# Spreading a weight load over every fourth partition, with a half-made table, shared buffers and new instruction orders, in a two-layer spectral and mixer kernel

## The chip, the cores and the metric

The kernel runs on one core of one Trainium2 chip. The metric is the device time of one execution in microseconds (us). "Span" is the time from the first to the last instruction in a trace. In every execution for which both are on record the time is 1.7 to 2.2 us longer than the span. A kernel is timed several times, and each call of the experiments ran its kernels and the kernel before on the same chip. All timed runs here are in the fast state.

## The reference, cut to what matters

```python
def _A_ref(x, w_r, w_i):                  # x: 1 x 2048 x 512, w: 2048 x 257
    X = rfft2(x)                          # over the 2048 rows and the 512 columns
    return irfft2(X * (w_r + 1j * w_i))

def _B_ref(x, w1, w2, w3, w4):
    h = _gelu(_layernorm(x) @ w1)         # 512 x 512
    # ... four column groups of h shifted by -1, +1, -2, +2 rows ...
    x1 = x + hs @ w2
    return x1 + _gelu(_layernorm(x1) @ w3) @ w4      # 512 x 1792 and back

for _ in range(2):                        # written out twice in the original
    x = x + _A_ref(_layernorm(x), A_w_r, A_w_i)
    x = x + _B_ref(_layernorm(x), B_w1, B_w2, B_w3, B_w4)
```

All inputs are bf16. Both layers use the same weights.

## The kernel before

Each FFT is a chain of matmuls with constant tables. A layer runs through these stages, and three lists of short names fix the order in which they are issued. A name is an operation, an index, sometimes the engine of the eviction (the copy of a matmul's result out of PSUM, where the matmuls here write their `ps` tiles; A = ScalarE, V = VectorE), and after the dot a PSUM bank.

- front (`O`): transform over 128 points within the 2048, with the rows' 1/std folded into the table `Tq = T * rstd` (`Q`).
- `d`: transform of the 512 columns. `q`: the other factor of the 2048 rows, with the table `TL`. `p`: the weighing, VectorE products of `X` and `W` into buffers `PB`. `b`: the inverse of `q` with `TR`, evicted into `M`.
- `D`: inverse of `d`. `P`: inverse of the front. Then the mixer: `v`, `u` (w1, w2), `w`, `W` (w3, w4).

The weights `w_r` and `w_i` must lie on 128 partitions as two forward and two reversed copies. The kernel before loads 64 partitions and copies them to the other 64:

```python
def load_W(K, w, pl, lo, hi):
    v = w.rearrange("(m j) f -> m j f", j=64)[:, :, 1:257]
    j1 = max(lo, 1)
    K.nc.sync.dma_start(K.W[0:32, pl, lo:hi], v[:, lo:hi])
    K.nc.sync.dma_start(K.W[32:64, pl, j1:hi], v[:, 65 - hi:65 - j1][:, ::-1])
    # ...
    K.later.append(lambda: K.nc.gpsimd.dma_start(K.W[64:128, pl, lo:hi], K.W[0:64, pl, lo:hi]))
```

The squares for the layer norms write their unused full result to one single buffer, and the sum of squares comes from the accumulator:

```python
    def square(self, i, src):
        junk = K.stream.tile([P, D], BF16, name="junk", bufs=1)
        K.nc.scalar.activation(junk[:], src, ACT.Square, bias=0.0, scale=D ** -0.5, accum_out=self.s[:, i, 1:2])
```

The scaled tables of the front go to VectorE only where the letter is V:

```python
def scaled_T(K, q, r, eng="V"):
    K.Tq[q] = K.stream.tile([P, 2, P], BF16, name="Tq", bufs=12)
    if eng == "V":
        K.nc.vector.tensor_scalar(K.Tq[q][:], K.T[:], r, None, op0=ALU.mult)
    else:
        K.nc.scalar.activation(K.Tq[q][:], K.T[:], ACT.Copy, bias=0.0, scale=r)
```

While the first data are on their way, 44 matmuls on zeros (`WAKE = 44`) keep TensorE busy, from 1.01 to 8.01 us in the first profile.

Of the kernel before, what the change touches and what calls it, by code (L numbers as in the profile page):

```python
# [23 lines left out]
SLAB = 130  # L24
# [3 lines left out]
def dft_tables():  # L28
# [55 lines left out]
    TL = np.concatenate([-B, A, B], axis=3).transpose(1, 2, 0, 3).reshape(P, NB, 192)  # L84
# [3 lines left out]
    TR = TR.reshape(NH, P, 2, 64).transpose(1, 2, 0, 3)  # L88
# [63 lines left out]
def load_all(K, A_x, A_w_r, A_w_i, B_w1, B_w2, B_w3, B_w4):  # L152
# [15 lines left out]
    K.TL = K.const.tile(list(tabs["TL"].shape), BF16, name="TL")  # L168
    K.TR = K.const.tile([P, 3, NH, 64], BF16, name="TR")
    load_q = lambda k, sl: nc.sync.dma_start(getattr(K, k)[:, sl], dram[k][:, sl])  # L170
    load_q("TL", slice(0, 8))
    K.W = K.const.tile([P, 2, NH, 256], BF16, name="W")
    K.later = []
    for lo in range(0, NH, 8):
        for pl, w in enumerate((A_w_r, A_w_i)):
            load_W(K, w, pl, lo, lo + 8)
        if lo == 8:
            load_q("TL", slice(8, 16))
        if lo in (0, 16):
            nc.sync.dma_start(K.TR[:, 0:2, lo:lo + 16], dram["TR"][:, :, lo:lo + 16])  # L180
# [4 lines left out]
    def load_mlp():  # L185
        gate2 = K.const.tile([1, 16], BF16, name="gate2")
        nc.sync.dma_start(gate2[:], K.W[64:65, 1, NH - 1, 0:16])
        for k, w, n, c in (("w1", B_w1, 4, D), ("w2", B_w2, 4, D), ("w3", B_w3, 4, FH), ("w4", B_w4, 14, D)):
            t = K.const.tile([P, n, c], BF16, name=k)
            nc.sync.dma_start(t[:], w.rearrange("(t p) n -> p t n", p=P))  # L190
            setattr(K, k, t)
# [8 lines left out]
def load_W(K, w, pl, lo, hi):  # L200


    v = w.rearrange("(m j) f -> m j f", j=64)[:, :, 1:257]
    j1 = max(lo, 1)
    K.nc.sync.dma_start(K.W[0:32, pl, lo:hi], v[:, lo:hi])
    K.nc.sync.dma_start(K.W[32:64, pl, j1:hi], v[:, 65 - hi:65 - j1][:, ::-1])
    if lo == 0:
        K.nc.sync.dma_start(K.W[32:64, pl, 0], v[:, 32])
    K.later.append(lambda: K.nc.gpsimd.dma_start(K.W[64:128, pl, lo:hi], K.W[0:64, pl, lo:hi]))


def make_hT(K):
    K.hT = K.big.tile([P, 4, NQ * SLAB], BF16, name="hT")
    hv = K.hT[:].rearrange("p i (q c) -> p i q c", c=SLAB)
    K.nc.gpsimd.memset(hv[:, :, :, 0:1], 0.0)
    K.nc.gpsimd.memset(hv[:, :, :, SLAB - 1:SLAB], 0.0)
# [18 lines left out]
class Stats:  # L235
# [18 lines left out]
    def square(self, i, src):  # L254

        K = self.K
        junk = K.stream.tile([P, D], BF16, name="junk", bufs=1)
        K.nc.scalar.activation(junk[:], src, ACT.Square, bias=0.0, scale=D ** -0.5, accum_out=self.s[:, i, 1:2])  # L258
# [45 lines left out]
    def mean(self, i, src):  # L304
        K = self.K
        junk = K.stream.tile([P, D], BF16, name="junk", bufs=1)
        K.nc.scalar.activation(junk[:], src, ACT.Copy, bias=0.0, scale=1.0 / D, accum_out=self.s[:, i, 0:1])
# [83 lines left out]
def first_front(K):  # L391
# [44 lines left out]
    for f in K.later:  # L436
# [4 lines left out]
def layer(K, last):  # L441
# [5 lines left out]
    PB = K.grp.tile([P, 8, 2, 2, 256], BF16, name="PB", tag="gT")  # L447
    n_pab = [0]
    M = K.grp.tile([P, 2, 2, NQ, P], BF16, name="M", tag="gT")
    xn = K.big.tile([P, NQ, D], BF16, name="xn", tag="V_xn")  # L450
    hv = K.hT[:].rearrange("p i (q c) -> p i q c", c=SLAB)
    ps = {}
# [13 lines left out]
    def take_d(u, eng):  # L466
        n = len(UNITS[u])
        tv[u] = K.stream.tile([P, n, 512], BF16, name="TV", tag="TV_Y", bufs=3, padded_shape=[P, 2, 512])
# [7 lines left out]
    def over_q(u):  # L476
# [5 lines left out]
        for i, b in enumerate(bs):  # L482
            for t in range(2):
                for h in range(2):
                    r = slice(64 * h, 64 * h + 64)
                    nc.tensor.matmul(o[:, h, i * 256:(i + 1) * 256], lhsT=K.TL[r, b, 64 * (1 - t):64 * (3 - t)],  # L486
# [6 lines left out]
    def weigh(u):  # L493
# [3 lines left out]
        for pl in range(2):  # L497
            t = PB[:, n_pab[0] % 8]
            n_pab[0] += 1
            w = K.W[:, pl, 2 * u:2 * u + 2 * n].rearrange("p (n h) f -> p h n f", h=2)  # L500
# [28 lines left out]
    def take_D(m, eng):  # L529
        Y[m] = K.stream.tile([P, 2, 512], BF16, name="Y", tag="TV_Y", bufs=3, padded_shape=[P, 2, 512])  # L530
# [18 lines left out]
    def stats2(q):  # L549
        ln[q // 4].square(q % 4, K.x[:, q, :])  # L550
# [29 lines left out]
    def gelu1(k):  # L580
        g, h = divmod(k, 2)
        o = ps.pop(("v", k))
        for i in range(2):
            nc.scalar.activation(hv[:, 2 * h + i, 4 * g:4 * g + 4, 1:P + 1],  # L584
                                 o[:, i].rearrange("p (q c) -> p q c", q=4), ACT.Gelu_apprx_tanh, bias=0.0, scale=1.0)

    def w2(n):
        q = ROWS[n]
        ps["u", n] = o = banks(K, 1)[:, 0]
        for j, dq in enumerate((-1, 1, -2, 2)):  # L590
            qq = (q + dq) % NQ
            st = SLAB * qq + 1 + (q + dq - qq) // NQ
# [79 lines left out]
    def take_front(k, eng):  # L672
# [3 lines left out]
        if k < PLAIN:  # L676
            if eng == "A":
                ps["right", k] = K.stream.tile([P, 2, 256], FP32, name="right", tag="TV_Y", bufs=3)
# [6 lines left out]
    def permute(k):  # L685

        w = K.W[:, k // 8, 4 * (k % 8):4 * (k % 8) + 4]
# [9 lines left out]

    next_V = {}
    table = {"d": over_d, "t": take_d, "q": over_q, "x": take_q, "p": weigh, "b": back_q,
# [29 lines left out]
s0 s3 s2 s4 i0 i2 s1 s5 s6 f4 i3 i4 S0 s9 s10 J0 S4 i10 s13 s7 Q0V J4 Q2A f5 s8 O0 i7 Q1A Q3A i9 Q4A i8 S5 s11 S1  # L729
s12 G0A O1 J1 i11 i12 Q5V G1A J5 Q9V Q6V Q13V Q10V s14 S2 s15 O2 Q7V O6 Q8V i15 J2 i14 Q12V G2A G6A Q11V O4 S3 J3  # L730
Q15V O3 Q14V G4A O5 G3V O7 G5A O8 G8A G7V
"""
ORDER_A = """
d1.0 d0.1 d4.2 t1A t0V q0.0 x0V q1.4 d6.6 x1V t4A p0 d2.0 t6A q4.4 d10.2 t2V q6.6 x4A p1 N0 p4 d8.4 t10A t8V x6A p6
q2.0 b1.2 b4.3 m1A d12.6 b0.2 m4A d14.3 x2A q10.4 t12A p2 d15.0 b5.1 t14V x10A m0V q8.6 b2.3 b6.4 x8A m2A m6A m5A
q12.6 q14.2 N1 p10 b7.5 t15A p8 b10.4 m7V b11.1 b3.0 x12A m11A x14V p12 p14 m3A b8.5 m8A q15.6 m10A b9.2 x15A p15
b12.3 b13.5 m12A m9A b14.4 m13V b15.3 m15V m14A m15A D0.2 D1.4 Y1A Y0V D3.6 P1.2 P0.3 P2.4 a1 P3.5 Y3A a0 a2 a3
D2.6 D4.2 Y2V P6.4 s1 P7.5 a6 a7 s0 P4.6 s2 P5.7 D7.0 s3 a5 a4 D5.4 r0 Y4A n2V s6 P8.7 s7 s5 P9.6 n3V s4 D6.2 Y7A
n1V a8 Y5A n0V Y6A P10.7 r1 P11.4 a9 P13.5 a10 P15.6 T1 n5V T0 n4V n6A P12.7 n7V s10 a11 T2 T3 a12 s9 a15 P14.2 s11
s8 a13 s13 s15 v0.0 c1 v1.4 a14 v3.2 s14 s12 r2 r3 c0 h1 n10V h0 v2.4 n11V h3 n9V T5 h2 n8V u0.2 n13V L3 n12A u1.3  # L740
u2.4 n14A n15A T4 f0 v5.0 h5 T6 v4.6 E0 u3.2 f1 L5 f2 c2 u4.3 h4 L7 f3 k1 T7 E3 k2 u5.6 f4 k0 k3 R0 f5 v7.4 v6.6
L13 E2 h7 u15.4 u7.5 k4 E1 f15 h6 o3V E4 u6.6 o0V E15 o1V k15 f6 u12.4 u11.7 f7 c3 f11 U0 o2A u8.6 k6 f8 u13.5 E5
f13 k5 E11 u9.7 E8 k7 k8 u10.6 u14.5 k11 R1 U1 f9 E6 f12 f10 w6.2 o6A f14 E12 E7 E9 k10 L2 o5V w0.6 w3.4 L8 k9 E10
o7V g0 R2 w5.6 k12 w4.0 E13 o4A k13 U2 g3 g4 w1.4 o9A E14 g1 o11V L15 w2.0 L6 L1 g5 k14 g2 R3 U3 w7.4 g6 w9.6 g7 L9
w8.2 w10.4 g9 L12 o15A o8V W0.6 o12A g8 W3.7 o10V w12.2 A0 w13.0 L11 o13A W1.6 g13 g12 g10 A3 U4 o14V A1 w11.2 g11
U5 w14.6 B3 W5.2 W7.3 W2.4 B0 A5 W4.2 L4 B5 A7 j3 j0 L14 B7 B1 W6.3 U7 A2 w15.4 A4 j1 g14 w17.6 g15 B2 A6 j5 j2
w16.4 g16 U6 B6 B4 S0 Q1 w20.2 w18.4 g18 L0 g17 j7 w19.0 g20 w21.4 j4 j6 S1 Q7 Q2 g19 Q3 w24.2 Q4 w22.0 g21 O1.4
G1A W9.6 g24 w26.2 g22 Q0 Q5 Q6 A9 G1V B9 w25.6 j9 w23.4 g26 g25 W10.6 W11.7 A10 g23 O3.4 G3A A11 B11 O2.2 L10 j11
w27.0 B10 G3V W8.6 A8 B8 g27 j8 j10 W15.7 A15 W13.6 S2 O0.4 Q9 W12.7 G2A Q10 B15 G2V Q11 A13 G0A Q8 G0V W14.6 j15
B13 O4.4 j13 A12 O5.2 S15 B12 Q15 S13 j12 O15.7 S12 Q13 Q12 G4A A14 B14 j14 G15V S14 Q14 G5A X4.0 O6.0 X4.6 O14.6  # L750
G6A G4V G15A G14A X8.2
"""
ORDER_B = """
d15.0 t15A d4.2 q15.0 x15V d1.4 t4A d8.6 t1A q1.4 q4.2 p15 t8A x1V b15.0 d12.6 x4A p1 m15V m15A q8.4 t12A d10.0
q12.6 p4 x8A b1.2 d2.4 t10V p8 q10.0 x12A d6.6 p12 m1A t2A x10A d0.3 t0V q2.4 t6A x2A b9.2 p10 b5.0 d14.1 q6.6 m9A
b4.3 t14V p2 b8.4 x6A b13.1 m4A b10.5 p6 q0.6 m5A b2.2 b12.3 x0A m10V q14.6 b11.0 b6.5 p0 m13A x14A m8A b3.1 m12A
p14 m3A b7.4 m6A b14.3 b0.1 m2V m14A m7V m0A m11V D3.0 Y3V D2.2 D1.4 Y2A P7.0 P6.1 P5.2 P4.3 Y1A a7 D0.4 s7 D5.6 a6
a5 P3.2 s6 a4 P2.3 Y0V P1.4 s5 a3 s4 P0.5 r1 a2 D6.0 a1 a0 Y5A n6V n7V s3 D4.2 n5V T3 P11.4 s2 n4V s1 s0 P10.5 D7.6
r0 Y4A a11 Y6A P9.2 P8.3 T2 a9 a8 n2V P13.4 Y7A n3V n1V a10 s9 P14.2 P12.3 s8 n0A c1 c0 P15.6 a13 v3.0 a15 v2.6 s11
T1 a12 s10 T0 r2 v1.4 s13 a14 s15 n11V s14 s12 h2 n10V v0.6 n9V h3 h1 T5 n8V T4 h0 r3 n13V u3.4 u2.5 n14V u0.6 n15V  # L760
n12V u1.7 f0 v5.0 f1 f3 f2 E1 v4.6 T6 c2 h5 T7 v7.0 k0 E3 E0 h4 h7 k3 u5.6 k2 u7.7 c3 E2 v6.0 k1 R0 f5 f7 u4.6 h6
u8.7 f4 k7 o3V u6.0 u12.1 o2A f8 E4 f6 u15.6 u14.7 o1V E8 o0A u9.0 f9 f14 E9 U1 k8 U0 u10.4 u13.5 f15 k4 k5 f10 f13
u11.0 f12 w0.2 k6 k14 w3.4 k9 E5 R1 k10 f11 w1.0 E6 o5V k13 E12 k11 w2.6 E11 R2 E15 k12 E7 o7V g0 k15 w6.2 o6V U3
g3 o11V g2 E10 R3 w4.6 g1 w5.0 o4V g6 o10A U2 w7.2 g5 g4 w12.0 g7 w11.2 w8.6 o15A o8V g8 g12 g11 W0.4 w13.0 w10.2
w9.6 W3.5 g10 E14 g13 o9V g9 W2.6 W6.7 o14A U4 U7 A2 W4.6 o12V W7.0 U5 A0 E13 A3 o13V W1.1 A6 U6 w14.4 w19.2 A4
w17.6 A1 g14 W5.1 A5 g17 y2 y4 w21.6 w15.4 g15 y3 g21 A7 w20.0 g19 w26.4 w16.2 g26 w24.4 w27.6 g24 g20 g16 w22.4
w18.2 w25.0 y7 g22 g18 W8.2 g25 y1 g27 w23.6 A8 W9.3 g23 W12.2 W11.6 W15.7 A12 y8 y5 A9 y9 W14.2 y6 A11 W13.3 y11
# [32 lines left out]
```

## Time and profile before

| | before |
|---|---|
| time, median of 3 runs | 362.52 us (361.94 to 364.64) |
| span of the profiled execution | 356.5 us, granted TensorE clock 1.000 |
| first front matmul / first `d` / last copy of W lands / first `D` | 9.78 / 19.89 / 36.88 / 42.48 us |
| first `d` / first `D` of layer two | 191.69 / 212.34 us |

I call the stretches between these marks the front (9.78 to 19.89), d-q (to the first `D`), mid (to layer two's first `d`), layer two's d-q, and the end. They cut the span into pieces that can be compared between kernels. The marks come from the traces by the first instruction of each kind on TensorE, and from the landing times of the DMA copies. The prediction below shows the profile's lines. In them PE is TensorE, PEld its weight loads, DVE VectorE, ACT ScalarE and POOL GpSimd; a bracket at the end of a line gives the idle time of the engine before it and what ended that.

### The profile page before, as it was taken

How to read it: one execution, taken by the hardware profiler on the slowest of the kernel's cores; microseconds unless marked ns; L12 is line 12 of the kernel's file. 1: busy time of each engine (PE TensorE's matmuls, PEld its weight loads, DVE VectorE, ACT ScalarE, POOL GpSimd, SP SyncE). 2: the span in 40 equal slices, each digit the busy share in tenths (PEclk: the TensorE clock that was granted, in tenths of full speed). 3: DMA queues.
4: the chain of work that ended last, by engine and by line, in shares of the span. 5: the costliest groups of instructions: out<-in, count | busy, mean ns of one | idle time of the engine just before them, and what ended most of it. 6: DMA issues, size and time to landing. Idle time of an engine off the chain costs nothing.

```text
span 356.5 us, 5618 instructions
## 1 busy us (share of the span) xinstructions
PE 341.2 (96%) x2124; PEld 187.6 (53%) x2124; DVE 182.9 (51%) x453; ACT 200.0 (56%) x343; POOL 66.1 (19%) x171
## 2 busy tenths in 40 slices
PE   7899898899999999999999999899999999999996
PEld 6767685344444444445457778544444444444442
DVE  5868897569933265131786979654860031100122
ACT  7979699986791411642207979958784500247100
POOL 1211036633310001100120003862250000000000
PEclk9999999999999999999999999999999999999999
DMA  7999696423330300000000000760340032000012
GB/s 250 273 250 214 220 318 118 83 38 59 60 61 4 85 2 0 0 2 1 0 2 0 2 2 2 120 118 2 59 88 3 0 65 69 0 29 2 29 44 88
DMA packets 47274, 24.60 MB, mean 69 GB/s; under 512 B 34832, under 2 KB 44048, under 8 KB 47248
## 3 DMA queue, kind: packets, MB, share of 16 engines
q1 hardware_dynamic: 46464, 22.09, 26.6%
q0 software_dynamic: 640, 2.10, 2.5%
q8 instruction: 16, 0.26, 0.3%
q10 hardware_dynamic: 144, 0.07, 0.1%
q14 instruction: 10, 0.08, 0.1%
HBM read 11.67 MB, written 2.10 MB: 39 GB/s over the span
## 4 chain that ended last, share of the span: by engine, by line
PE 75%; ACT 10%; DMA 9%; DVE 2%; issue 2%; SPq 1%; ACTq 0%; DVEq 0%; POOLq 0%
PE ps L641 27%; PE ps L628 27%; PE ps L593 7%; PE ps L577 5%; ACT junk L258 4%; DMA W<-in_A_w_i_dram 3%; PE ps L462 2%; DMA W<-W 2%; DMA TL<-tab_TL 2%; ACT Y L149 2%; PE ps L526 2%; PE ps L510 1%; ACT M L149 1%; DMA W<-in_A_w_r_dram 1%; PE ps L486 1%
## 5 line engine op out<-in xcount | busy, mean ns | idle before, releaser
L635 ACT ACTIVATE gT<-ps 128x1024 bf16<-128x1024 f32 x56 | 54.6, 1024 | 81.7 <-PE ps L628 71.9
L641 PE MATMUL ps<-w,gT 128*128 128x512 bf16 x448 | 98.7, 379 | 0.0
L628 PE MATMUL ps<-xT,w 128*128 128x512 bf16 x448 | 98.5, 379 | 0.0
L646 DVE TENSOR_TENSOR x_state<-ps,x_state 128x512 bf16<-128x512 f32 x32 | 21.8, 690 | 125.4 <-PE ps L641 125.2
L628 PEld LDWEIGHTS <-w 128*128 128x128 bf16 x448 | 43.8, 98 | 52.6
L641 PEld LDWEIGHTS <-gT 128*128 128x128 bf16 x448 | 43.8, 98 | 52.4
L577 PE MATMUL ps<-xT,w 128*128 128x512 bf16 x128 | 29.1, 379 | 2.8 <-DMA xT<-xn 1.5
L601 DVE SCALAR_TENSOR_TENSOR xn<-xn,ln_c,ps 128x512 bf16<-128x512 bf16 x32 | 22.9, 745 | 13.1 <-PE ps L593 5.1
L593 PE MATMUL ps<-w,hT 128*128 128x512 bf16 x128 | 28.8, 379 | 0.3 <-ACT hT L584 0.2
L258 ACT ACTIVATE junk<-x_state 128x512 bf16<-128x512 bf16 x36 | 22.6, 629 | 1.5 <-DVE x_state L546 0.4
L258 ACT ACTIVATE junk<-xn 128x512 bf16<-128x512 bf16 x32 | 20.1, 627 | 6.0 <-DVE xn L601 5.5
L546 DVE SCALAR_TENSOR_TENSOR x_state<-ps,x_state 128x512 bf16<-128x512 f32 x32 | 20.4, 687 | 4.3 <-PE ps L538 4.3
L501 DVE TENSOR_TENSOR PB<-X,W 128x1024 bf16<-128x1024 bf16 (+1 forms) x40 | 21.2, 578 | 2.1 <-issue 1.3
L577 PEld LDWEIGHTS <-w 128*128 128x128 bf16 x128 | 12.3, 98 | 18.1 <-issue 2.4
L584 ACT ACTIVATE hT<-ps 128x512 bf16<-128x512 f32 x32 | 17.6, 608 | 6.5 <-PE ps L577 6.4
L593 PEld LDWEIGHTS <-hT 128*128 128x128 bf16 x128 | 12.5, 98 | 15.8 <-ACT hT L584 0.9
L246 DVE BATCH_NORM_STATS2 ln_st<-x_state 128x6 f32<-128x512 bf16 x28 | 18.5, 680 | 3.7 <-DMA x_state<-in_A_x_dram 3.6
L281 POOL TENSOR_SCALAR ln_ve<-ln_mv 128x4 f32<-128x4 f32 (+1 forms) x15 | 3.9, 261 | 79.3 <-DVE ln_mv L274 78.6
L510 PE MATMUL ps<-TR,PB 128*128 128x128 bf16 x256 | 17.1, 219 | 1.3 <-DVE PB L501 0.9
L462 PE MATMUL ps<-FA,V 128*128 128x256 bf16 x128 | 16.3, 273 | 0.9 <-ACT V L149 0.7
L538 PE MATMUL ps<-Y,Tinv 128*128 128x256 bf16 x128 | 15.5, 272 | 1.6 <-ACT Y L149 1.6
L526 PE MATMUL ps<-G,M 128*128 128x256 bf16 x128 | 15.4, 273 | 1.5 <-ACT M L149 0.9
(73 smaller groups left out, 378.6 us busy)
## 6 DMA issues: line engine op xcount, KB each, us to landing
w<-in_B_w_dram SPq DMA_DIRECT2D x2, 1792.0 KB, 12.5
x_state<-in_A_x_dram SPq DMA_DIRECT2D x8, 256.0 KB, 4.7
W<-W POOLq DMA_DIRECT2D x8, 256.0 KB, 8.2
out_dram<-x_state SPq DMA_DIRECT2D x16, 128.0 KB, 1.8
TR<-tab_TR SPq DMA_DIRECT2D x2, 512.0 KB, 8.8
w<-in_B_w_dram SPq DMA_DIRECT2D x2, 512.0 KB, 5.1
W<-in_A_w_r_dram SPq DMA_DIRECT2D x7, 128.0 KB, 8.8
W<-in_A_w_i_dram SPq DMA_DIRECT2D x7, 128.0 KB, 8.2
```

What stands on the lines that cost most here:

```text
L258: K.nc.scalar.activation(junk[:], src, ACT.Square, bias=0.0, scale=D ** -0.5, accum_out=self.s[:, i, 1:2])
L462: nc.tensor.matmul(oi[:, 1 - h], rhs=K.FA[:, t, h], lhsT=V[:, 2 * t + h, 2 * b:2 * b + 2].rearrange("d b q c -> d (b q c)"), start=(t == 0 ...
L501: nc.vector.tensor_tensor(t[:, :, 0:n], x, w, op=ALU.mult)
L510: nc.tensor.matmul(o[:, (2 * h + F) * P:(2 * h + F + 1) * P], lhsT=pab[u][k][:, h, b - u, F * P:(F + 1) * P], rhs=K.TR[:, k:k + 2, 2 * b + ...
L526: nc.tensor.matmul(o[:, i, e * 256:(e + 1) * 256], lhsT=M[:, F, e, 2 * m + i, :], rhs=K.G[:, F, e, :], start=(F == 0 and e == 0), stop=(F ...
L577: nc.tensor.matmul(o[:, i], lhsT=K.w1[:, t, j * P:(j + 1) * P], rhs=xT[g][:, :, t, :], start=(t == 0), stop=(t == 3))
L593: nc.tensor.matmul(o, lhsT=K.hT[:, j, st:st + P], rhs=K.w2[:, j, :], start=(j == 0), stop=(j == 3))
L601: nc.vector.scalar_tensor_tensor(xn[:, q, :], xn[:, q, :], ln[q // 4].c[:, q % 4:q % 4 + 1], ps.pop(("u", n)), op0=ALU.mult, op1=ALU.add, ...
L628: nc.tensor.matmul(o[:, i], lhsT=K.w3[:, c, t * P:(t + 1) * P], rhs=xT3[g][:, :, c, :], start=(c == 0), stop=(c == 3))
L635: nc.scalar.activation(gT[g][:, 2 * j:2 * j + 2, :], ps.pop(("w", k)), ACT.Gelu_apprx_tanh, bias=0.0, scale=1.0)
L641: nc.tensor.matmul(o, lhsT=gT[g][:, t, i * P:(i + 1) * P], rhs=K.w4[:, t, :], start=(t == 0), stop=(t == 13))
L646: nc.vector.tensor_tensor(K.x[:, q, :], ps.pop(("W", n)), K.x[:, q, :], op=ALU.add)
```

## The change

Its intent is to bring the weights in sooner, to spend less DMA on a table, to free buffers, and to use all that with new orders.

```diff
-SLAB = 130
+SLAB = 136
+PAD = 4
 ...
-    v = w.rearrange("(m j) f -> m j f", j=64)[:, :, 1:257]
+    v = w.rearrange("(m j) f -> m j f", j=64)
     j1 = max(lo, 1)
-    K.nc.sync.dma_start(K.W[0:32, pl, lo:hi], v[:, lo:hi])
-    K.nc.sync.dma_start(K.W[32:64, pl, j1:hi], v[:, 65 - hi:65 - j1][:, ::-1])
+    fwd, rev = [K.W[2 * sg::4, pl] for sg in range(2)]
+    K.nc.sync.dma_start(fwd[:, lo:hi], v[:, lo:hi])
+    K.nc.sync.dma_start(rev[:, j1:hi], v[:, 65 - hi:65 - j1][:, ::-1])
 ...
-    K.later.append(lambda: K.nc.gpsimd.dma_start(K.W[64:128, pl, lo:hi], K.W[0:64, pl, lo:hi]))
+    if pl == 1:
+        K.later.append(lambda: K.nc.gpsimd.dma_start(K.W[1::2, :, lo:hi], K.W[0::2, :, lo:hi]))
+
+def turn_TL(K, sl):                       # the half of TL that is no longer loaded
+    old, new = [K.TL[:, sl, k].rearrange("p b (c h) -> p b c h", h=2) for k in range(2)]
+    K.nc.gpsimd.tensor_scalar(new[:, :, :, 0], old[:, :, :, 1], -1.0, None, op0=ALU.mult)
+    K.nc.gpsimd.tensor_copy(new[:, :, :, 1], old[:, :, :, 0])
 ...
-        junk = K.stream.tile([P, D], BF16, name="junk", bufs=1)
+        if out is None:                   # else: xn[:, q, :]
+            out = K.stream.tile([P, 1, D], BF16, name="junk", tag="TV_Y", bufs=4, padded_shape=[P, 2, 512])[:, 0]
 ...
-    PB = K.grp.tile([P, 8, 2, 2, 256], BF16, name="PB", tag="gT")
-    M = K.grp.tile([P, 2, 2, NQ, P], BF16, name="M", tag="gT")
+    PB = [K.grp.tile([P, 7, 2, 2, 256], BF16, name="PB", tag="gT") for _ in range(2)]
+    M = hv[:, :, :, PAD:PAD + P].rearrange("p (F e) q c -> p F e q c", F=2)
 ...
-        tv[u] = K.stream.tile([P, n, 512], BF16, name="TV", tag="TV_Y", bufs=3, ...)
+        tv[u] = K.stream.tile([P, n, 512], BF16, name="TV", tag="TV_Y", bufs=4, ...)
 ...
+    def gelu_table(_):                    # "z0" in the order of layer one
+        t = K.small.tile([P, 1], FP32, name="wake")
+        nc.scalar.activation(t[:], K.eps[:], ACT.Gelu_apprx_tanh, bias=0.0, scale=1.0)
 ...
-s0 s3 s2 s4 i0 i2 s1 s5 s6 f4 i3 i4 S0 s9 s10 J0 S4 i10 s13 s7 Q0V J4 Q2A f5 s8 O0 ...
+s0 s2 s1 s3 i3 s5 f4 i0 i2 s4 i4 S0 s7 J0 Q0P s6 Q3V Q4V s8 s10 S4 J4 i7 O1 Q2A O0 ...
 ... (all three order lists are new)
```

The product's operand becomes `K.W[..., 1:257]`, because whole rows of 257 columns are loaded now.

> **What bounds the kernel now.** I read the page first: how busy TensorE is, and when DMA is full.
>
> ```profile
> span 356.5 us, 5618 instructions
> PE 341.2 (96%) x2124; PEld 187.6 (53%) x2124; DVE 182.9 (51%) x453; ACT 200.0 (56%) x343; POOL 66.1 (19%) x171
> ...
> PE   7899898899999999999999999899999999999996
> ...
> DMA  7999696423330300000000000760340032000012
> GB/s 250 273 250 214 220 318 118 83 38 59 60 61 4 85 2 0 0 2 1 0 2 0 2 2 2 120 118 2 59 88 3 0 65 69 0 29 2 29 44 88
> ```
>
> TensorE is busy for 341.2 of 356.5 us, so about 15 us of plain gaps can be won, less what no order removes: the start before the first data and the last store. The timed 362.5 us is 6 us over the span; I keep that difference. DMA is loaded only in the first six slices (53 us). A table of stages, bounded by the first instruction of each kind on PE, shows where the gaps are.
>
> ```profile
> 8.00:9.78 1.78, 0.02 (x2) 0.00 (x1) 1.78 (x8) 1.73 (x7) 0.20 (x1) 1.00 0.98 328
> 9.78:19.89 10.11, 9.05 (x81) 7.73 (x80) 8.17 (x30) 8.90 (x17) 2.73 (x6) 1.00 1.14 263
> 19.89:42.48 22.59, 20.34 (x256) 15.72 (x257) 18.85 (x33) 19.19 (x26) 2.04 (x4) 1.00 0.92 208
> 42.48:61.84 19.36, 17.89 (x144) 14.01 (x145) 14.58 (x42) 16.72 (x37) 8.56 (x24) 1.00 0.83 243
> 191.69:212.34 20.65, 19.79 (x256) 15.29 (x257) 16.88 (x30) 18.45 (x27) 0.00 (x0) 1.00 0.01 2
> 212.34:232.00 19.66, 17.98 (x145) 13.98 (x145) 14.76 (x42) 17.21 (x38) 10.32 (x29) 1.00 0.34 55
> ```
>
> Columns: stretch, its us, busy us and count of PE, PEld, DVE, ACT, POOL, then clock, DMA share, GB/s. Rows three and five are the same work (forward d, q, inverse q: 256 matmuls) in layers one and two: 22.59 us with DMA at 0.92, 20.65 us with DMA at 0.01. So loading costs layer one at most **1.94 us**. From 88.3 to 188.0 the same table gives PE 99.70 of 99.70 us: the MLP cannot be shortened, and nothing in the change touches its 448 matmuls of 98.7 us per line. The chain of waits inside row three names the load:
>
> ```profile
> 26.64 6.80 DMA W<-W
> 33.44 0.61 DVE PB L501
> 34.05 1.33 issue
> 35.38 0.70 DVE PB L501
> ...
> 42.48 2.88 PE ps L526 x24
> ```
>
> DVE waits 1.33 us for weights that are copied from the lower to the upper 64 partitions. The timelines of ACT and PE show a second, separate loss:
>
> ```profile
> 63.06 1.28 ACT L584 ACT_TABLE_LOAD   x1
> ```
>
> ```profile
> 65.01 1.24 PE L577 MATMUL ps<-xT,w 128*128 128x512 bf16 x5 [1.28 <-ACT hT L584]
> ```
>
> The first gelu loads its table while PE waits for the banks that gelu should free: 1.28 us of PE, in layer one alone.
>
> [...] in a table of 4 us windows the 128-partition x load runs at 353 GB/s (6 to 10 us), while the time in which W goes to 32 partitions and then across runs at 218 to 262 (10 to 34 us). [...] the 128x1024 product takes 684 ns with aligned W. [...]
>
> **The change part by part.**
>
> W: 16 main loads write strided partitions; the forward half becomes runs of 8 x 257 x 2 = 4112 B in place of eight of 512 B; the reversed half keeps rows (514 B). Eight copies of 256 KB become four for both planes. TL from HBM falls from 768 to 512 KB. Between 10 and 36 us some 6.2 MB move (sum of window times rate). At an assumed 330 GB/s, between 245 now and 353 seen, 5.9 MB need 18 us in place of 24, so the last copy, now landing near 36.9 us, should land near 30. That removes most of the 1.94 us: **-1.6**.
>
> TL's other half: four GpSimd instructions of 512 elements[...]. GpSimd is 2.04 us busy in the 22.59 us of row three and idle in layer two's stage, and TL's first part lands near 11.5 us while q starts at 21.9. Hidden, unless the pair for the second half, which waits for TL's second load (it lands at 20.4 us), delays the second W copy queued behind it.
>
> Weighing with W at an odd element: 40 products, 21.2 us. [...] **0**. [...]
>
> M in the padded hT, PB with 14 buffers for 8, TV_Y with 4 for 3, squares written to xn or TV_Y: no instruction more. They free waits of tenths. They let the new orders place work, worth counting only there.
>
> Gelu table early: issued just after the last inverse-q evictions, when ACT waits for the inverse d anyway: **-1.2** of the 1.28.
>
> Order of the first front: now S0 comes after three ACT statistics (s1 s5 s6), then after two. One s is about 1.5 us, so the first matmul moves from 9.78 to about 8.3. But Q letters: four of 16 on ACT now. The new list has two A and seven P; the helper tests only for V, so **P also means ACT**: nine. Five more at 0.42 us (four take 1.69 us) is +2.1 us on ACT. ACT's sum becomes: four s at 1.5, nine Q at 0.41, six S at 0.24, five double evictions at 0.96, two single at 0.55, together 17 us from 3.75 us, so V is complete near 21 in place of 19.8 if ACT never waits, nearer 20 with overlaps. I count **+0.6**.
>
> Layer two's d/q stage by letters, with the row durations (ACT double 1.03 to 1.16, single 0.6 to 0.68, M 0.61; DVE double 1.28, single 0.7, products 11.6 in all): ACT 22.2 to 20.8, DVE 18.8 to 20.0. Better balanced: **-0.7**. In layer one the sums stay (ACT 20.5, DVE 21).
>
> Inverse d and p stages, 19.4 and 19.7 us, hold some 14 us of matmuls of 0.109 us; 16 squares of 0.73 and six or eight Y of 1.0 bind ACT, 16 adds of 0.7 and the norms bind DVE. New letters shift a few: **-0.4** each, -0.8. The end of the second front: before, three ACT evictions (1.79 us) follow the last fronts; now G6 comes earlier: **-0.4**.
>
> Sum: -1.6 - 1.2 + 0.6 - 0.7 - 0.8 - 0.4 = **-4.1**, so 362.5 - 4.1 = **358.4 us**.
>
> **Rivals.** (1) The start eats the gain: ACT becomes the bound of the first front and d begins 1.7 us later; the sum above speaks for it, the earlier S0 against. With W hidden anyway, since d starts later, about 361. (2) [...] (3) The orders fit the new buffers so well that nearly all avoidable gaps go: PE has 2.2, 1.5, 0.9 and 1.7 us of gaps in rows three to six, plus 1.8 in row one, and stretched matmuls besides; that gives 354 to 355. (4) The transfers don't speed up[...]: then -1.6 becomes 0 and the total is 360.
>
> **Range and chances.** The pieces have independent errors of about 1 us (front) and 0.5 to 0.8 us (the others), so some 2 us together, plus 0.7 for the spread of runs (361.94 to 364.64): 8 in 10 between 354.8 and 361.6. A 2% gain needs 355.3 or less, near the low end: 0.14. A 2% loss needs rival 2: 0.02.
>
> **What would show it.** Last W copy landing near 30 us and 300 GB/s or more between 10 and 28 us: part one right. A table load before the Y evictions and no 1.28 us gap at the first gelu: part two. First d matmul at 20 to 21 us with ACT gapless before it: the P reading; at 19 or less: wrong. Product of 128x1024 still near 684 ns: alignment harmless. Layer two's d/q stage at 20 us. The prediction fails if front, d/q and d/p stages all shrink by 2 us, or if GpSimd delays the copies past the need.

## The result

| | before | after |
|---|---|---|
| time, median of 4 runs | 363.33 us (361.94 to 364.64) | 354.12 us (353.63 to 354.35) |
| span of the profiled execution | 356.5 us | 352.1 us |

The ratio of after to before is 0.9754 (95% interval 0.9717 to 0.9791): faster by over 2%. The ratios here are the record's own, from the fast runs of both kernels, and are not quite the ratios of the medians. The result lies below the predicted range.

One thing stands out at once. The times differ by 9.2 us and the two profiled spans by 4.3 us (356.45 and 352.13 before rounding). The page of the kernel after, its head and the rows of slices:

```profile
span 352.1 us, 5565 instructions
PE 338.8 (96%) x2103; PEld 188.2 (53%) x2124; DVE 184.5 (52%) x442; ACT 200.5 (57%) x355; POOL 68.2 (19%) x171
...
PE   7889899999999999999999999999999999999996
...
DMA  7995926611030030300000000663003005101003
GB/s 245 267 335 197 383 88 120 119 32 30 1 61 0 0 61 13 76 0 2 1 2 0 2 2 2 121 106 64 11 7 85 0 0 106 45 0 47 0 30 104
```

Slices three and five move 335 and 383 GB/s, where no slice of the kernel before passed 318, and the sixth slice is already down to 88 GB/s: the load of the tables and of W is over. The five stretches of the kernel after, in the columns that the prediction explains (us, then busy us and count of PE, PEld, DVE, ACT, POOL, then clock, DMA share, GB/s):

```profile
8.87:21.15 12.28, 9.78 (x80) 7.69 (x79) 9.64 (x28) 12.23 (x29) 4.72 (x7) 1.00 0.95 282
21.15:42.06 20.91, 19.61 (x257) 15.90 (x257) 18.68 (x34) 19.13 (x27) 3.15 (x5) 1.00 0.81 298
42.06:189.15 147.09, 145.23 (x774) 74.93 (x785) 87.00 (x222) 75.17 (x134) 32.92 (x82) 1.00 0.19 41
189.15:208.99 19.84, 19.02 (x258) 15.95 (x256) 17.80 (x30) 17.45 (x27) 0.00 (x0) 1.00 0.01 2
208.99:352.10 143.11, 138.56 (x694) 68.58 (x704) 47.03 (x116) 71.88 (x128) 25.87 (x68) 1.00 0.21 45
```

In the front ACT is busy for 12.23 of 12.28 us, so ACT sets its length. Between the two profiles the first front matmul comes 0.91 us earlier, the front gets 2.18 us longer, d-q 1.69 shorter, mid 2.11, layer two's d-q 0.82 and the end 0.97 shorter. That is 4.3 us. It accounts for the spans, and it leaves 4.9 us of the timed difference unexplained. The experiments start there.

### The profile page after: what moved, and what is told of

Its sections match the earlier page's. It is cut to its first block, busy times and chain, and to the rows that moved or that the text cites. A ratio compares the mean times of both kernels' runs of the same rounds, so it can differ in the third digit from the quotient of the medians.

```text
span 352.1 us, 5565 instructions
## 1 busy us (share of the span) xinstructions
PE 338.8 (96%) x2103; PEld 188.2 (53%) x2124; DVE 184.5 (52%) x442; ACT 200.5 (57%) x355; POOL 68.2 (19%) x171
## 3 DMA queue, kind: packets, MB, share of 16 engines
q0 software_dynamic: 576, 2.11, 1.5%
## 4 chain that ended last, share of the span: by engine, by line
PE 77%; ACT 8%; DMA 6%; DVE 4%; issue 3%; SPq 1%; POOL 1%; DVEq 0%; POOLq 0%; ACTq 0%
PE ps L655 26%; PE ps L642 26%; PE ps L591 8%; PE ps L607 8%; ACT hT L151 2%; PE ps L540 2%; PE ps L552 2%; DMA xT<-xn 2%; DMA W<-W 2%; PE ps L476 1%; DMA x_state<-in_A_x_dram 1%; ACT gT L649 1%; DVE PB L515 1%; ACT X L151 1%; DMA W<-in_A_w_i_dram 1%
## 5 line engine op out<-in xcount | busy, mean ns | idle before, releaser
L649 ACT ACTIVATE gT<-ps 128x1024 bf16<-128x1024 f32 x56 | 56.5, 1023 | 84.2 <-PE ps L642 81.1
L655 PE MATMUL ps<-w,gT 128*128 128x512 bf16 x433 | 97.7, 379 | 0.8
L276 POOL TENSOR_SCALAR ln_mv<-ln_s 128x4 f32<-128x4 f32 x16 | 5.5, 344 | 91.1 <-DVE x_state L560 52.1
L591 PEld LDWEIGHTS <-w 128*128 128x128 bf16 x128 | 12.3, 98 | 15.8 <-issue 1.2
L270 ACT ACTIVATE xn<-x_state 128x512 bf16<-128x512 bf16 x32 | 19.7, 620 | 0.5 <-DVE x_state L560 0.2
L540 PE MATMUL ps<-G,hT 128*128 128x256 bf16 x128 | 15.1, 273 | 2.1 <-DVE hT L149 1.2
L524 PE MATMUL ps<-TR,PB 128*128 128x128 bf16 x256 | 16.0, 219 | 0.0
```

Source lines behind the costliest of these rows:

```text
L270: K.nc.scalar.activation(out, src, ACT.Square, bias=0.0, scale=D ** -0.5, accum_out=self.s[:, i, 1:2])
L540: nc.tensor.matmul(o[:, i, e * 256:(e + 1) * 256], lhsT=M[:, F, e, 2 * m + i, :], rhs=K.G[:, F, e, :], start=(F == 0 and e == 0), stop=(F ...
L591: nc.tensor.matmul(o[:, i], lhsT=K.w1[:, t, j * P:(j + 1) * P], rhs=xT[g][:, :, t, :], start=(t == 0), stop=(t == 3))
L649: nc.scalar.activation(gT[g][:, 2 * j:2 * j + 2, :], ps.pop(("w", k)), ACT.Gelu_apprx_tanh, bias=0.0, scale=1.0)
L655: nc.tensor.matmul(o, lhsT=gT[g][:, t, i * P:(i + 1) * P], rhs=K.w4[:, t, :], start=(t == 0), stop=(t == 13))
```

## The experiments

Eighteen runs were made, three of them repeats of a kernel that had run, all with correct results. "Same call" means the same chip and shared runs of the kernel before.

### What does the timed kernel before look like?

**The kernel before again**, unchanged, with a new profile.

> The kernel before, unchanged, against itself, for the span of every timed run. Theory 1 (the profile of before is a lucky execution, and the timed ones lose 4 to 5 us more, most of it in the loading of W): spans of 359 to 362 us, some 2 us under the time, varying by 1 us or more, and the loss lies before the inverse d of layer one, at 45 us or later in place of 42.48. Theory 2 (before has a constant 6 us between span and time, after has 2): spans near 356.5 us beside times of 362 to 364. Ratio 1.00 in both.

It took 364.06 us (ratio to the kernel before of the same call 1.001 [0.9966, 1.0055]), and its new profile has a span of 361.7 us. So the first profile was an execution some 5 us faster than this one. The five stretches of this run:

```profile
12.21:24.60 12.39, 11.66 (x80) 8.96 (x80) 8.28 (x30) 9.19 (x17) 2.76 (x6) 0.77 1.00 202
24.60:47.73 23.13, 20.44 (x256) 15.77 (x257) 18.85 (x33) 19.21 (x26) 2.06 (x4) 1.00 0.83 191
47.73:196.93 149.20, 146.01 (x785) 74.68 (x785) 85.26 (x220) 78.66 (x136) 33.90 (x82) 1.00 0.23 55
196.93:217.59 20.66, 19.80 (x256) 15.30 (x257) 16.88 (x30) 18.45 (x27) 0.00 (x0) 1.00 0.01 2
217.59:361.70 144.11, 139.01 (x704) 68.61 (x704) 48.24 (x124) 67.70 (x120) 25.78 (x68) 1.00 0.21 44
```

The last three rows repeat the first profile to 0.05 us. Everything that differs lies before 47.73 us. DMA moved 202 GB/s in the front instead of 263. The third piece of x landed at 7.85 us instead of 5.31, and the last copy of W at 41.85 instead of 36.88. The clock in the front was 0.77. TensorE's timeline shows a gap before it:

```profile
12.21 0.37 PE L349 MATMUL ps<-Tq,x_state 128*128 128x256 bf16 x1 [4.67 <-DVE Tq L336]
```

TensorE had idled for 4.67 us, and its records show half clock from 11.0 us for 6.8 us (mean clock 0.88, 0.50 and 0.77 in the 4 us windows from 8 to 20 us): successive matmuls started 0.21 us apart there and 0.11 us apart later. By the mean clocks of their stretches, the half clock lasted some 3.4 us in after_old_orders (0.85 over 11.65 us), after_old_order0 (0.85 over 11.29 us) and before_long_wake (0.94 over 26.35 us), and some 6.8 us in sched_only (0.87 over 25.84 us) and after_short_wake. The traces give no length of gap from which it follows: after a gap of 2.24 us (after_fewer_bufs) and one of 2.42 us (after_TL_loaded) successive matmuls started 0.21 us apart from 10.89 and 11.25 us on, after one of 2.02 us (runs_only) eight matmuls of line 486 took 1.03 us instead of 0.61, and after one of 2.44 us (data_only_fit) matmuls started 0.11 us apart.

The five calls list span and clock of each timed run. The 61 runs of the kernel before, these six included, have spans of 358.7 to 364.9 us, median 361.1, and 59 of them a granted clock below 0.9995; the two at 1.000 have spans of 359.2 and 360.6 us. None is as short as 356.5 us. Time minus span is 2.05 to 2.17 us in each. So the kernel before was profiled in a rare good execution. The kernel after repeats: 352.1, 351.7, 352.4 and 352.3 us in its first four runs.

### Is it the dip of the clock, or the load?

Two kernels set the clock theory against the load theory: the kernel before with more of the matmuls on zeros, and the kernel after with fewer.

```diff
-WAKE = 44
+WAKE = 68        # kernel before: "before_long_wake"
+WAKE = 20        # kernel after:  "after_short_wake"
```

> Before with 68 wake matmuls for 44, so that PE works until about 11 us in place of 7.5. Theory (the timed runs of before lose to a half granted clock that follows PE's 4.7 us gap before the first real matmul, not to the late data alone): the half-clock stretch at 11 us goes, granted clock 0.995 or more, 361 to 361.5 us (6.8 us at half clock held some 4.5 us of matmuls, about 2.3 us lost). Rival (the late data alone sets the front): no change, 363.5 us.

> After with 20 wake matmuls for 44, so that PE idles from about 4 to 8.9 us: a positive control. Theory: the granted clock falls to 0.5 for 3.4 or 6.8 us in the front, mean 0.991 to 0.995, and the time goes from 354.1 to 355.5 to 357 us. Rival: no change.

The long wake gave 364.62 us, ratio 1.0036 [0.9988, 1.0083], no gain:

```profile
12.13:22.22 10.09, 9.05 (x80) 7.71 (x80) 8.17 (x30) 8.88 (x17) 2.22 (x5) 1.00 1.05 200
22.22:48.57 26.35, 21.65 (x256) 16.89 (x257) 19.01 (x33) 19.14 (x26) 2.54 (x5) 0.94 0.86 190
```

The front ran at full clock and took 10.09 us instead of 12.39, so `d` began 2.4 us earlier than in the repeat above. But the first `D` came at 48.57 us, not earlier than 47.73. VectorE's timeline names what was waited for:

```profile
40.61 1.90 DVE L501 TENSOR_TENSOR PB<-X,W 128x1024 bf16<-128x1024 bf16 x3 [2.72 <-DMA W<-W]
```

That wait ended with a copy that landed at 40.53 us; the last one landed at 42.04. A late W takes back what an early front gives. TensorE idled for 2.30 us before 41.36, and a new half-clock stretch of some 3.4 us followed at 43.0 (eight matmuls of line 510 took 1.01 us at 43.16 and 0.61 at 33.30). My theory that the clock dip of the front costs the kernel before its 5 us fell.

The short wake took 355.68 us (ratio 0.9793 [0.9756, 0.983]; 353.75 us for a near copy of the kernel after in the same call, spread_only below). TensorE idled for 3.58 us and ran at half clock for 6.8 us (mean clock 0.94, 0.50 and 0.70 in the 4 us windows from 4 to 16 us), but the front grew from 12.29 to only 12.64 us, because ACT sets its length (busy for 7.90 us from 8 to 16 us), and `d` began at 21.09 us as without the dip. The dip isn't what costs time here: the two timed runs at a granted clock of 1.000 took 355.70 and 355.53 us, like the others. In its profile the loss lies in the mid stretch, 147.82 us against 146.51 in spread_only: the first `v` matmul waits 1.18 us for a transposing DMA (`xT<-xn`), which the kernel after's profile has with 0.45 us. Whether the short wake has to do with that, I can't say.

### The layout of W: partitions or run length?

The change alters two things of the W load at once: the partitions it reaches and the length of its runs. **spread_only** is the kernel after with spread partitions but short rows. **runs_only** is the kernel before with whole rows of 257 columns but its old partitions. The two ask which of these W waited for.

```diff
 # spread_only, from the kernel after
-    v = w.rearrange("(m j) f -> m j f", j=64)
+    v = w.rearrange("(m j) f -> m j f", j=64)[:, :, 1:257]
 # runs_only, from the kernel before
-    v = w.rearrange("(m j) f -> m j f", j=64)[:, :, 1:257]
+    v = w.rearrange("(m j) f -> m j f", j=64)
```

> After with W on every fourth partition as in after, but rows of 512 B (columns 1 to 256) in place of 4112 B runs. [...] last W copy near 31 us, 354 to 355 us. If the length of the runs is: last copy near 37 us or later, 357 us or more.

> Before with all 257 columns of W loaded (forward half in runs of 4112 B), on the old contiguous partitions. [...] the last W copy stays at 40 to 42 us and the time at 363 us. If the length of the runs is: the last copy comes 3 us or more earlier and the time falls below 361 us.

They ran in one call. spread_only took 353.75 us (ratio 0.9745), with its last copy of W at 31.1 us. runs_only took 365.34 us (1.005 [1.0, 1.0101]), with its last copy at 45.7 us. So the gain of the layout doesn't come from the long runs. The rate of all DMA in windows of 4 us (the last figure, GB/s) shows the difference, first the kernel after, then before_again:

```profile
22.00:26.00 4.00, 4.00 (x43) 2.87 (x42) 3.08 (x6) 3.58 (x4) 1.69 (x3) 1.00 1.00 353
24.00:28.00 4.00, 3.29 (x32) 2.59 (x33) 1.83 (x4) 2.61 (x4) 0.00 (x0) 1.00 1.13 235
```

So rival 4 of the prediction, no faster transfers, is out, and my reading, that the partitions set the rate, fits this. It isn't isolated: with the spread come four copies of 512 KB in place of eight of 256 KB, and no run changes only one of the two.

### Data without orders, orders without data

**sched_only** is the kernel after with the old load of W and the old tables. **after_old_orders** is the kernel after with the three old order lists. **data_only_fit** is the kernel before with the new load of W, the new tables and the squares written to `xn` or the shared buffers. To make room in SBUF `Tq` has 10 buffers instead of 12 there.

```diff
 # sched_only: W[0:32], W[32:64] and eight copies as before, TL and TR as before
 # after_old_orders: ORDER_0, ORDER_A, ORDER_B of the kernel before
 # data_only_fit, from the kernel before, besides load_W, TL and TR (stats2's squares go to xn):
-        junk = K.stream.tile([P, D], BF16, name="junk", bufs=1)
+            out = K.stream.tile([P, 1, D], BF16, name="junk", tag="TV_Y", bufs=3, ...)[:, 0]
-    K.Tq[q] = K.stream.tile([P, 2, P], BF16, name="Tq", bufs=12)
+    K.Tq[q] = K.stream.tile([P, 2, P], BF16, name="Tq", bufs=10)
```

> After with the old W and TL (32 and 64 contiguous partitions, rows of 512 B, TL wholly from HBM, eight copies), everything else of the change kept. Theory 1 (the data part is worth some 6 us when the kernel is timed): 359 to 361 us, ratio to before 0.99. Theory 2 (the data part is worth 1.7 us, the orders and buffers the rest): 355 to 357 us, ratio 0.98.

> After with all three old orders (so without the early gelu table), the data part and the buffers kept. Theory 1: 356 to 358 us, ratio 0.983, as the data part alone brings about 6 us. Theory 2: 360 to 362 us, ratio 0.995.

> Before with the new W layout and the half-made q table alone: old orders, M and 8 product buffers as before, 3 TV_Y. (To make room, squares go to xn or TV_Y and the scaled tables have 10 buffers for 12.) If the late W copies are what the timed runs of before lose: as with all buffers (358.0 us), 357.5 to 358.7 us. If the gain of the data part needs the buffers as well: 360 us or more.

| | time, us | ratio to before, same call | front, us | d-q, us | mid | layer two's d-q | end |
|---|---|---|---|---|---|---|---|
| sched_only | 363.16 | 0.9982 [0.9948, 1.0017] | 12.27 | 29.83 | 146.51 | 19.82 | 143.37 |
| after_old_orders | 358.03 | 0.9837 [0.9801, 0.9874] | 11.65 | 21.55 | 148.08 | 20.66 | 143.73 |
| data_only_fit | 358.39 | 0.9889 [0.9868, 0.9909] | 9.99 | 21.72 | 148.09 | 20.66 | 144.07 |

The new orders and buffers without the new load give nothing: the 4.3 us that they win after the first `D` (149.20 + 20.66 + 144.1 becomes 146.51 + 19.82 + 143.37) are lost before it, where d-q takes 29.83 us. The chain of waits of sched_only says why:

```profile
23.08 13.47 DMA W<-in_A_w_r_dram
...
37.10 5.29 DMA W<-W
...
42.60 2.72 PE ps L512 x24
```

A load of W takes 13.47 us, the copy to the upper partitions another 5.29, and then TensorE, idle for 4.71 us before line 512, runs at half clock for 6.8 us (mean clock 0.87 from 22.16 to 48 us). The data without the orders give 3.8 us (362.19 less 358.39), and with the buffers 5.4 (363.46 less 358.03); most of that step is the kernel before, whose median was 1.3 us higher in the second call, and the stages of the two kernels' profiles differ by no more than 0.4 us from the first `D` on and 0.2 in d-q. Together data and orders give 9. The orders' gain shows in the time only once W is on time.

One part of the orders pays even with the old load. In sched_only x's third piece landed at 7.74 us, as late as in before_again (7.85), and yet TensorE began at 9.88 us instead of 12.21, without a dip in the front:

```profile
9.88 0.27 PE L351 MATMUL ps<-Tq,x_state 128*128 128x256 bf16 x1 [1.74 <-DVE Tq L338]
```

### Are the new buffers part of it?

**after_fewer_bufs** takes both new sets of buffers away from the kernel after, **after_PB7** only the second tile of products, **after_TV3** only the fourth shared buffer.

```diff
 # after_PB7
-            t = PB[n_pab[0] % 14 // 7][:, n_pab[0] % 7]
+            t = PB[0][:, n_pab[0] % 7]
 # after_TV3, at all five places
-            tag="TV_Y", bufs=4
+            tag="TV_Y", bufs=3
```

> After with 3 TV_Y buffers for 4 and 7 product buffers for 14, orders kept. If the buffers are what lets the new orders work: 1 us or more slower, 355 us and above, with waits of DVE on PE before products. If not: within 0.4 us of after.

> After with 7 product buffers for 14, TV_Y with 4. If the products' buffers are what counts: 360 to 362 us, PE waiting for products in both layers. If not: 354 to 355 us.

> After with 3 TV_Y buffers for 4, products with 14. If the products' buffers are what made fewer buffers 8 us slower: within 0.7 us of after (354.0 to 354.8). If TV_Y's: 357 us or more.

after_fewer_bufs took 362.0 us (0.9988 [0.9947, 1.003]), after_PB7 361.34 us (0.9973 [0.9938, 1.0008]), after_TV3 354.93 us (0.979 [0.9767, 0.9813]). Seven product buffers instead of 14 cost the new orders some 7 us: d-q takes 26.79 us, and layer two's 22.06 instead of 19.84. TensorE's timeline of after_PB7:

```profile
31.82 0.62 PE L524 MATMUL ps<-TR,PB 128*128 128x128 bf16 x8 [1.77 <-DVE PB L515]
...
36.35 2.74 PE L524 MATMUL ps<-TR,PB 128*128 128x128 bf16 x24 [2.50 <-DVE PB L515]
```

TensorE waits for products. VectorE in its turn waits 0.45 us for line 524 to read an old product at 32.55 us, at a place where the kernel after has no wait. A half-clock stretch of 3.4 us follows in this profile (24 matmuls of line 524 took 2.74 us at 36.35 and 1.51 at 41.28), but the three timed runs at a granted clock of 1.000 took 360.2 to 360.6 us too. The fourth shared buffer shows in d-q alone, 21.92 us instead of 20.90. The kernel before had eight product buffers, so this says what the new orders need, not what the old ones lacked.

### The smaller parts

**after_no_z** drops the early load of the gelu table. **after_TL_loaded** loads both halves of `TL` and makes nothing on GpSimd. **after_old_order0** uses the old order of the first front. **after_P_as_V** turns the P letters of its Q operations into V, which moves seven scaled tables from ScalarE to VectorE.

```diff
 # after_no_z
-... m15A m15V D1.1 D0.5 z0 L13 Y1V ...
+... m15A m15V D1.1 D0.5 L13 Y1V ...
 # after_TL_loaded: the table in DRAM holds both halves
-            turn_TL(K, slice(8 * k, 8 * k + 8))
 # after_P_as_V
-... J0 Q0P s6 Q3V ... Q1P ... Q8P ... Q7P ... Q11P ... Q6P ... Q14P ...
+... J0 Q0V s6 Q3V ... Q1V ... Q8V ... Q7V ... Q11V ... Q6V ... Q14V ...
```

> After without the early gelu table load. Both theories: the table load returns to the first gelu and costs PE 1.2 us there, so 355.3 us against 354.1; if the load then falls where ACT has slack, no change.

> After with both halves of the q table (1 MB) loaded from HBM and no GpSimd work on it. If making half of it on GpSimd matters: the last W copy moves from 31 to 33 us or later and the time from 354.1 to 355 us or more. If it does not: within 0.4 us of after, as W is no longer what the stage waits for. Beside that: if the third x piece lands at 7.2 us or later again (as it did in the kernels with the old W and TL on these chips: 7.25 to 7.85, against 5.5 to 6.4 with the new), the size or place of the tables has to do with it; if at 6.4 us or before, the layout of W has.

> After with the old order of the first front alone. By the front of the profiles (old orders with the new data: first d matmul at 22.4 us with a half-clock stretch; new: 21.15 at full clock): 355 to 355.5 us, granted clock below 1.0 in most runs. If the new front order costs more than it brings, as I predicted from one profile (+0.6 us): 353.5 us.

> After with the seven P of the first front, which run on ACT, put on VectorE. If ACT is what ends the front (12.23 us busy of 12.28 before the first d): the first d matmul comes 1 us or more earlier and the time falls to 353.0 to 353.5 us. If DVE then ends it: no change or slower.

In the profiles before and after, ScalarE's second table load, of 1.28 us, comes before its first gelus. after_no_z took 355.64 us (ratio 0.9773), 1.5 us more than the kernel after had in its own runs, which were another call. Its trace has the table load at 60.46 us, just before the first gelus, and its mid stretch is 147.94 us, where the kernel after had 147.09 and, in its repeat below, 146.51. TensorE waits for the gelus for 0.43 and 0.59 us, which it doesn't in the kernel after:

```profile
62.41 1.89 PE L591 MATMUL ps<-xT,w 128*128 128x512 bf16 x8 [0.43 <-ACT hT L598]
...
65.83 2.75 PE L607 MATMUL ps<-w,hT 128*128 128x512 bf16 x12 [0.59 <-ACT hT L598]
```

In the kernel after, the load stands at 41.56 us, ahead of the inverse `d` (ScalarE's timeline):

```profile
41.56 1.28 ACT L715 ACT_TABLE_LOAD   x1
```

after_TL_loaded took 354.18 us (ratio 0.9768), which is no difference from 354.12. GpSimd's work on `TL`, 4.8 us in four instructions, is hidden (GpSimd's timeline of the kernel after):

```profile
12.79 1.66 POOL L219 TENSOR_SCALAR TL<-TL 128x512 bf16<-128x512 bf16 x1
14.36 0.76 POOL L220 COPY TL<-TL 128x512 bf16<-128x512 bf16 x1
15.05 0.87 POOL L213 DMA_DIRECT2D W<-W  x1
20.18 1.65 POOL L219 TENSOR_SCALAR TL<-TL 128x512 bf16<-128x512 bf16 x1 [4.26 <-DMA TL<-tab_TL]
21.74 0.76 POOL L220 COPY TL<-TL 128x512 bf16<-128x512 bf16 x1
22.41 0.68 POOL L213 DMA_DIRECT2D W<-W  x1
```

The second W copy does queue behind the second pair, as the prediction feared: it goes at 22.41 us. In after_TL_loaded the last copy landed at 34.37 us, 12.3 us after the first `d` instead of 9.7, and d-q is 20.90 us all the same. So W has at least 2.6 us to spare in the kernel after.

after_old_order0 took 354.87 us (ratio 0.9802) in the same call, 0.7 us more than after_TL_loaded (the runs of the two overlap), and all its runs show a granted clock of 0.990 to 0.995: its first front matmul waits until 10.91 us. The new order starts earlier for the same x. In before_again and after_TL_loaded the third piece of x landed at 7.85 and 7.69 us, and the first front matmul came at 12.21 and 9.84 us.

after_P_as_V took 353.26 us. Its front is 10.95 us instead of 12.29, so ScalarE was the bound there and P does mean ScalarE. Its d-q is 21.48 us instead of 20.90, so VectorE takes part of it back.

### A version that beats both

**best** combined what looked good: P as V, short rows of spread W, and `WAKE = 50`. **after_again** and **P_as_V_again** repeat the kernel after and the single-letter change in one call.

> After with what the runs spoke for: the P of the first front on VectorE, W in rows of 512 B (spread_only, no slower), 50 wake matmuls for 44 to close PE's gap before the first real one. 352.5 to 353.3 us, granted clock 1.0 in every run.

> The changed kernel, unchanged, on the same chip and in the same rounds as P_as_V_again. By its record 353.6 to 354.4 us, spans 351.7 to 352.4 us at granted clock 1.0, some 2 us under the time, the last W copy landing near 31 us.

> After with the seven P of the first front on VectorE, against after on the same chip. If the first run of it (353.3 us) was no luck of the chip: 0.6 to 1.2 us below after_again, the first d matmul some 1 us earlier. If it was: within 0.3 us of it.

best missed: 355.05 us (354.58 to 355.35), slower than the two of its parts that ran alone (353.26 and 353.75). Its d-q was 22.12 us. Its last copy of W landed at 32.6 us, but that of the two P-as-V runs, at 32.4 and 32.1, was no earlier. Whether the longer wake or the shorter rows with this front did it isn't settled. The repeats gave 354.02 us (353.39 to 355.3) for the kernel after, ratio 0.9716 [0.9666, 0.9766], and 352.63 us (352.26 to 353.18) for P as V, ratio 0.9674 [0.9621, 0.9728]. Their ranges don't overlap, and the profiled spans are 351.5 and 351.3 us. So P as V is the fastest version that ran, by 1.4 us of medians in that call. The two intervals overlap and the profiled spans differ by only 0.2 us, so the size of that lead is rough.

## Why the prediction was wrong

It said 358.4 us (354.8 to 361.6), and 354.12 came. By its own steps:

**The step that failed is "The timed 362.5 is 6 us over the span; I keep that difference."** The difference is 1.7 to 2.2 us in every execution, of either kernel, for which both are on record. The other 4 us were a difference between two executions: the profiled one, with a good start, and the timed ones, in which, going by before_again, x and W came late and the clock fell. The change brings W in sooner and starts sooner on a late x, so the 4 us must not be kept. With 356.5 - 4.1 + 2 the same sum would have said 354.4 us. That this lies so close is luck in part: against the 4.3 us between the two profiles the sum had the front 0.7 us too low, and the gelu table, D, P and the end together 0.7 us too small a gain. The clue was in the prediction: a gap of 6 us that nobody had explained is a quantity to be explained, and it could be part of what the change removes. Rival 3 gave "354 to 355", but for another reason, gaps closed by the orders. PE still has 2.5 us of gaps in the new front and 1.3 in d-q, so that isn't what happened.

**W (-1.6).** The transfers did speed up as predicted: 353 GB/s from 22 to 26 us, the last copy at 30.82 (said: near 30), and 300 GB/s or more in parts of the stretch. The size was wrong in both ways of looking. Between the profiles the load's share is about 0.9 to 1.0 us (d-q 22.60 becomes 21.55 and 21.72 with new data and old orders), and the orders gave another 0.7 in layer one, where I had said "the sums stay". For the timed executions the term was mis-sized the other way. From before_again to after the first `D` comes 5.7 us earlier: 3.34 from the first matmul, 0.11 from the front, 2.23 from d-q. Of the 3.34, the new front order has some 2.3 by sched_only (9.88 instead of 12.21), and the rest goes with x, whose third piece landed at 6.44 in the kernel after. The kernel before was held twice, by a late front and by a late W, and before_long_wake shows that mending the front alone gives nothing. "Loading costs layer one at most 1.94 us" held for one profile with the old orders; with the new orders the old load costs d-q 8.9 us (29.83 less 20.90).

**Gelu table (-1.2).** Right in size: after_no_z has 1.0 us of waits for the first gelus and a mid stretch 0.85 or 1.43 us longer than the kernel after's two profiles. Its 1.5 us of time is a comparison between calls.

**The front (+0.6).** The reading of P was right, and ScalarE became the bound. Between the profiles `d` begins 1.26 us later, against 0.6 predicted. Against the timed kind of execution it begins 3.4 us earlier (24.60 becomes 21.15), because the new order stands a late x. Rival 1, the start eats the gain, held in the one profile that I had, and not in the runs that count.

**Layer two's d-q (-0.7).** Measured -0.82. **D, P and the end of the second front (-0.8 and -0.4).** Mid shrinks by 2.1 us and the end by 0.97, together 3.08, of which the gelu table accounts for 0.85 to 1.43. That leaves 1.65 to 2.2 where I had 1.2.

**Buffers ("They free waits of tenths").** Right for the old orders: with and without the new buffers (after_old_orders and data_only_fit) d-q is 21.55 and 21.72 us, mid 148.08 and 148.09, the end 143.73 and 144.07. The prediction put no figure on what the new orders need of them: with seven product buffers instead of 14 they lose 7 us. And one buffer had a cost of its own that I had not seen. ScalarE's timelines, before and after, where squares follow each other:

```profile
60.81 0.63 ACT L258 ACTIVATE junk<-x_state 128x512 bf16<-128x512 bf16 x1
61.35 0.19 ACT L258 ACTIVATION_READ_ACCUMULATOR junk<-x_state 128x1 f32 x1
61.57 0.63 ACT L258 ACTIVATE junk<-x_state 128x512 bf16<-128x512 bf16 x1
```

```profile
50.26 0.61 ACT L270 ACTIVATE xn<-x_state 128x512 bf16<-128x512 bf16 x1
50.78 0.19 ACT L270 ACTIVATION_READ_ACCUMULATOR xn<-x_state 128x1 f32 x1
50.88 0.61 ACT L270 ACTIVATE xn<-x_state 128x512 bf16<-128x512 bf16 x1
```

Counted from the start of the accumulator's read, the next square starts 0.22 us later before, and 0.10 us later after. Over all 72 reads the medians are 217 and 93 ns. Before, the longer time stands only where one write to `junk` follows another, 50 times; where another output follows, it is 93 ns there too. That is 50 x 0.125, some 6 us of ScalarE, most of it beside other work. The medians of all four traces with the one buffer are 217 or 218 ns, and those of all others 93. Whether the chip or a semaphore of the program makes it isn't shown. With the old orders kept, mid fell from 149.20 to 148.09 us in data_only_fit, whose one edit of ScalarE's work in that stretch is where the squares write; its end, 144.07, did not fall. So I put about 1.1 us down to it, though no run changes that alone.

**GpSimd (hidden).** The four instructions took 4.8 us and were hidden. **Products with W at an odd element (0).** That this costs nothing was my estimate. It was right, and rival 2, a slower product, is out, by the view of the tile W in the kernel after, which lists minimum, median and maximum ns, then first and last start:

```profile
L515 DVE TENSOR_TENSOR PB<-X,W x40: 409/684/695, 24.2 to 206.6; 128x1024 bf16<-128x1024 bf16 x24, 128x512 bf16<-128x512 bf16 x16
```

The median is 684 ns, as with aligned W.

**What stays open.** I don't know why the first profile had a good start; its chip isn't on record. In the traces with W on the old partitions, x's third piece landed at 7.25 to 7.85 us in all but that first one (5.31). With W spread it landed at 5.5 to 6.6 us in all but after_TL_loaded (7.69), which loads more of `TL`. By what I had written down before that run, 7.69 us speaks for the size of the tables and not for the layout of W. It is one execution, and the first profile, with the old tables, had 5.31, so this stays open. That the timed runs before look inside like before_again is inferred from their spans and clocks.

## What to carry to other kernels

Compare the span of the profile with the spans of the timed runs before you add anything up: if the profile is of a better execution than the timed ones, the parts where executions differ are where the change may win most. A change can show nothing until another is made: the new orders alone gave 0.3 us of medians, the data alone about 4, both together 9; test the pair. Ask which partitions a load reaches (353 GB/s from 22 to 26 us with W on every fourth, against 178 to 235 in the 4 us windows from 16 to 36 us of before_again), and look at what a string of accumulating operations writes to: one throwaway buffer may not be free (217 ns from the accumulator's read to the next square here, against 93).
